# A fused attention and SwiGLU kernel: the output weights loaded by neighbouring rows, the wide weight columns in one transfer each, and a new order of work

## The chip, the core and the metric

The kernel runs on one core of a Trainium2 chip. A core has TensorE (PE, the matrix engine; its weight loads are listed apart, as PEld), VectorE (DVE), ScalarE (ACT), GpSimd (POOL) and SyncE (SP), which each run their own list of instructions in order and wait for each other by semaphores. Transfers between the chip's main memory and the core's on-chip memory are issued from SP, ACT or POOL and are carried out by 16 DMA engines. The metric is the device time of one execution in microseconds (us), lower being better.

## What is computed

For 8 batches and 8 heads, 576 positions and a head dimension of 64, attention with a forget gate; its result, rearranged to 4608 tokens of 512 values, goes through a gated feed-forward block of width 1536:

```python
log_f = np.log(np.clip(f, 0.0001, 1.0))
cum = np.cumsum(log_f, axis=-1)
scores = scale * q @ k.T + cum[..., :, None] - cum[..., None, :]
scores = np.where(causal, -1e9, scores)
attn = softmax(scores)                      # over the keys
x = (attn @ v) transposed and reshaped to (4608, 512)
g, val = x @ w_gate, x @ w_val              # (512, 1536) each
out = (g * sigmoid(g) * val) @ w_out        # (1536, 512)
```

Inputs and output are float32. The matrix products are done in bfloat16 with float32 sums.

## The kernel before

Attention works on pairs of heads (`p`, 32 of them), each in two halves `g` of query blocks (blocks 0 to 3, and 4 to 8, of 64 rows). For a pair, k and q are loaded, cast to bfloat16 (`kb`, `qb`), turned by TensorE (`tx`) and copied out (`kt`, `qz`). TensorE forms scores into `sp`; VectorE adds the forget sums `cb`, takes the row minimum and writes `t` and `tm` (L652); ScalarE takes the exponential (`e`, `eo`, L672); GpSimd, and for the first pairs ScalarE too, divides by the row sum and writes `pk` (L708); `pk` is turned into `pT`, for the first eight pairs by TensorE through a `gv` bank (L743), later by a DMA transpose; TensorE multiplies by v (`vt`, L764) and the result is copied, already transposed, into `xT`, the input of the feed-forward block.

The feed-forward block goes by tiles of tokens: two of 256 tokens, seven of 512, then 256, 128 and 128. `gate` (L839) makes, for each piece of a tile, a bank of gate columns from `wg` and one of value columns from `wv`, with 512 values in a bank; ScalarE takes a tanh (`th`, L855), VectorE makes the gated product `hh` in two passes (L857, L860). `project` multiplies `hh` with `wo` and stores 128 tokens at a time. Each matmul of 128 output rows is issued as two of 64 columns of the stationary operand (`columns`, L201), so a pair of matmuls, each with its own weight load of 64 columns, makes one product. The stationary operand of a gate product is the weight `wt[:, ko, fc * P:fc * P + P]`, 128 neighbouring columns; the moving operand is `xT`, 512, 256 or 128 tokens wide. In `project` the stationary operand is `hh` and the moving one is `wo[:, fc, :]`.

The weights lie in three on-chip arrays for the whole run. `weights` (L814) issues their loads from POOL, which also casts them to bfloat16: `wg` and `wv` in four pieces of columns each (0 to 256, to 512, to 1024, to 1536), `wo` in three pieces of 512 rows. A row `fc*128 + p` of `w_out` goes to partition `p` of chunk `fc`.

All of the order is fixed before the run. Every step is given to a planner (`Plan`) with the engines that may do it and a cost for each, a priority, buffers, and for transfers a DMA cost (`dma`) and a share of the DMA engines (`pk`). `Plan.order` simulates the engines with these costs and writes out the instructions of each engine in the order that it found. Several constants steer it: `STARTUP` is the sequence of the loads of the first part, `AHEAD` and `BEHIND` say how far apart in that sequence a load may be issued, `SLACK` how long a buffer is held for an earlier user, and `NUDGE` shifts the priorities of single units of work (a: scores and softmax, f: gates, o: projections, q: preparations, v: v loads). These are orders and not waits: the instructions that come out wait for their data only.

Of the kernel before, what the change touches and what calls it, by code (L numbers as in the profile page):

```python
# [197 lines left out]
def columns(nc, out, lhsT, rhs, **kw):  # L198
    for h in range(2):
        c = slice(64 * h, 64 * h + 64)  # L200
        nc.tensor.matmul(out[c, :], lhsT[:, c], rhs, **kw)  # L201
# [8 lines left out]
def mm(*cols):  # L210
    return sum(max(29, c / 2.4 + 2.5) for c in cols)
# [3 lines left out]
def kernel(  # L215
# [11 lines left out]
    nc = tc.nc  # L227
# [4 lines left out]
    P = 128  # L232
# [31 lines left out]


    NHALF = 4
    NSELA = 4
    NSEL = 1
    CUT = QB * (HI[0] + 1)
    MOST = (("p", 1), ("o", 2), ("f", 3))  # L270
    AHEAD = 10
    BEHIND = 5
    BOTH = 8
    LATER = {"DVE": 100}
    SPARE = {"ACT": 400, "DVE": 700}
    FREE = 8
    SLACK = 400
    SOON = 8
    BACK = 4
    CBACK = 5  # L280
    STARTUP = "p0 q1 f9 v01 k0 p2 wv2 q0 v04 wv0 wg2 wg0 k2 v00 c3 c1 q3 q2 wv4 v02 p4 c2 v03 c4 wg4 v11 c5 wv8 wg8 v10 v14 p5 v13 wo4 p6 v12 c6 wo0 c7 p7 wo8 c0"
    HEAD = "00 10 20 30 11 01 31 21"


    NUDGE = "a0.0:-6 a1.0:-12.5 a10.0:1 a10.1:1.5 a12.0:-0.5 a13.0:0.5 a13.1:-1 a15.0:-1 a15.1:1 a16.0:-3 a17.0:-2 a17.1:-1.5 a18.0:-0.5 a21.0:-1 a21.1:-1 a22.1:0.5 a25.1:-1 a26.1:-1.5 a27.0:-1.5 a27.1:1 a29.0:2 a30.1:-1 a31.0:0.5 a31.1:0.5 a4.0:2.5 a4.1:2.5 a5.0:-1.5 a5.1:-1 a6.0:0.5 a6.1:1 a7.1:-0.5 a8.0:-1 a9.1:-0.5 f0:4 f1:2 f11:-4 f3:-5 f4:-3.5 f5:-4 f6:-2 f7:1 f8:9.5 f9:0.5 o0:-1 o1:-991 o10:-12.5 o11:3.5 o4:1 o5:-7 o6:-4.5 o8:1 o9:9 q0:-8.5 q1:-12 q10:-1.5 q11:-3 q12:-1.5 q13:-3 q14:-4 q15:-2 q16:-6 q17:1.5 q18:-4 q19:-2 q2:-10 q21:0.5 q24:0.5 q26:2.5 q27:0.5 q29:-2 q3:-9.5 q30:-4 q4:-7 q5:-5 q6:-1 q8:-1 v1:-5.5 v2:-2 v3:3.5 v4:1.5 v5:5.5 v6:0.5 v7:-5"

    WAIT = ""
    ORDER = [(int(u[0]), int(u[1])) for u in HEAD.split()]
# [7 lines left out]
    pl = Plan()  # L296
# [14 lines left out]
    wo = sb.tile([P, KF, DM], BF16)  # L311
# [31 lines left out]
    pl.most = {("gv", x): n for x, n in MOST}  # L343
    pl.slack = SLACK

# [3 lines left out]
    for h in range(2):  # L349
        nc.gpsimd.affine_select(  # L350
            out=maskf[64 * h:64 * h + 64, :], in_=maskf[64 * h:64 * h + 64, :],
# [113 lines left out]
    def prepare(p):  # L465
        s = first[p]
        if p < NHALF:
            prepare_parts(p)
# [54 lines left out]
    def load_parts(p):  # L523
        b, hp = divmod(p, NPB)
        pl.key(("cb", p), "cb", p)
        for name, x, a, z, r, n in parts(p):
# [4 lines left out]
            def load(e, u, fk=fk, src=(k if name == "k" else q), a=a, z=z, r=r, m=m):  # L531
# [79 lines left out]
    def scores(p, g):  # L611
# [3 lines left out]
        for n, bank in enumerate(BANKS[g]):  # L615
# [4 lines left out]
            def mult(e, bank=bank, sk=sk):  # L620
                sp, kt, qz, o = pl.buf(sk), pl.buf(("kt", p)), pl.buf(("qz", p)), 0
                for i, a, z in bank:
# [148 lines left out]
    def spread(p, g, pv):  # L771
# [5 lines left out]
        for a, z in ((0, cut), (cut, w)):  # L777
# [3 lines left out]
            def evac(e, a=a, z=z):  # L781
# [4 lines left out]
                full = [list(d) for d in src.ap]  # L786
                x = R if p >= NHALF else R // 2
                inner = [[1, QB // x], [QB // x, x]]
# [28 lines left out]
    def weights():  # L817
        def piece(engs, fn, reads, writes, *a, **kw):
            loads[writes[0]] = pl.op(engs, fn, reads, writes, *a, **kw)

        cuts = [0, 256, 512, 1024, 1536]
        for a, z in zip(cuts, cuts[1:]):
            for nm, wt, src in (("wg", wg, moe_w_gate), ("wv", wv, moe_w_val)):
                piece({"POOL": 600}, lambda e, wt=wt, src=src, a=a, z=z: nc.gpsimd.dma_start(
                    out=wt[:, :, a:z], in_=src[:, a:z].rearrange("(ko p) n -> p ko n", p=P)),
                    (), [(nm, n) for n in range(a // P, z // P)], 2 + a / 256, dma=5.1 * (z - a) + 880, pk=20 if z - a == 256 else 42)
        for c in range(0, KF, 4):
            piece({"POOL": 600}, lambda e, c=c: nc.gpsimd.dma_start(
                out=wo[:, c:c + 4, :], in_=moe_w_out[c * P:(c + 4) * P, :].rearrange("(ko p) n -> p ko n", p=P)),
                (), [("wo", n) for n in range(c, c + 4)], 7 + c / 4, dma=3500, pk=42)  # L830

    gates_of = {}

    def gate(t, tok, n):
        nf = 512 // n
        x0 = tok % NRING
        assert x0 + n <= NRING
        for u in range(KF // nf):
            fcs = range(u * nf, u * nf + nf)  # L839
            xs = [("x", hp, m) for hp in range(KD) for m in range(tok // QB, (tok + n) // QB)]  # L840
            pr = 1000 + t * 20 + u
            for nm, wt in (("wg", wg), ("wv", wv)):
                bk = (nm, t, u)
                pl.key(bk, "gv", line="f")

                def mult(e, wt=wt, bk=bk, fcs=fcs):
                    for j, fc in enumerate(fcs):
                        for ko in range(KD):
                            columns(nc, pl.buf(bk)[:, j * n:j * n + n], wt[:, ko, fc * P:fc * P + P],
                                    xT[:, ko, x0:x0 + n], start=ko == 0, stop=ko == KD - 1)  # L850
                o = pl.op({"PE": mm(*[n] * (KD * nf))}, mult, xs + [(nm, fc) for fc in fcs], [bk], pr, lat=220)
                gates_of[t] = o
            pl.key(("th", t, u), "th")
            pl.key(("hh", t, u), "hh")
            pl.op({"ACT": 487}, lambda e, u=u: nc.scalar.activation(pl.buf(("th", t, u)), pl.buf(("wg", t, u)), AF.Tanh, scale=0.5),  # L855
                  [("wg", t, u)], [("th", t, u)], pr - 5000, lat=120)
            pl.op({"DVE": 605}, lambda e, u=u: nc.vector.scalar_tensor_tensor(  # L857
                pl.buf(("th", t, u)), pl.buf(("th", t, u)), 1.0, pl.buf(("wg", t, u)), op0=ALU.add, op1=ALU.mult),
                [("th", t, u), ("wg", t, u)], [("u", t, u)], pr - 5000, lat=180)
            pl.op({"DVE": 605}, lambda e, u=u: nc.vector.tensor_mul(pl.buf(("hh", t, u)), pl.buf(("th", t, u)), pl.buf(("wv", t, u))),  # L860
                  [("u", t, u), ("th", t, u), ("wv", t, u)], [("hh", t, u)], pr - 5000, lat=100)
# [41 lines left out]
    for b in range(B):  # L903
        pl.key(("vt", b), "vt")
        load_v(b)
    weights()
    line = []
    for x in STARTUP.split():
        n = int("".join(c for c in x if c.isdigit()))
# [95 lines left out]
```

## Time and profile before

| what | value |
|---|---|
| median of 3 runs | 414.49 us (414.43 to 421.14) |
| the profiled execution | 415.21 us |
| its span, from the first to the last instruction | 413.4 us |
| PE, DVE, ACT, POOL busy | 95%, 81%, 78%, 66% of the span |
| granted TensorE clock | 1.0 throughout |

The profiled execution is 1.8 us longer than its span, which is what lies before and after the instructions, and 0.7 us above the median. The views used here are the page of the whole run, tables of busy time in chosen stretches, the waits of one engine put down to what ended them, the chain of work that ended last, the groups of instructions by line and shape, and the timeline. In a group's row, "busy" is the time in which at least one of the group was running, and "mean ns" the mean length of one; since the two matmuls of a pair run side by side and are pipelined, busy time divided by the count is much less than the mean.

### The profile page before, as it was taken

How to read it: one execution, taken by the hardware profiler on the slowest of the kernel's cores; microseconds unless marked ns; L12 is line 12 of the kernel's file. 1: busy time of each engine (PE TensorE's matmuls, PEld its weight loads, DVE VectorE, ACT ScalarE, POOL GpSimd, SP SyncE). 2: the span in 40 equal slices, each digit the busy share in tenths (PEclk: the TensorE clock that was granted, in tenths of full speed). 3: DMA queues.
4: the chain of work that ended last, by engine and by line, in shares of the span. 5: the costliest groups of instructions: out<-in, count | busy, mean ns of one | idle time of the engine just before them, and what ended most of it. 6: DMA issues, size and time to landing. Idle time of an engine off the chain costs nothing.

```text
span 413.4 us, 15350 instructions
## 1 busy us (share of the span) xinstructions
PE 392.5 (95%) x5848; PEld 269.3 (65%) x5848; DVE 333.2 (81%) x1270; ACT 320.5 (78%) x904; POOL 271.1 (66%) x475
## 2 busy tenths in 40 slices
PE   3988988889999999999999999999999999999996
PEld 2667878777666765567776666665566555568775
DVE  4799987798999789999998999899989952775232
ACT  5799988799999998979998897998899653332221
POOL 7679966699996887799789798878777340000000
PEclk9999999999999999999999999999999999999999
DMA  7999979879799999999999999978996744000211
GB/s 192 190 216 226 216 126 247 163 189 210 184 230 191 229 196 233 241 203 230 224 196 223 234 210 225 239 215 182 201 223 114 149 93 126 2 2 28 79 53 52
DMA packets 144026, 72.16 MB, mean 175 GB/s; under 512 B 117904, under 2 KB 131728, under 8 KB 143952
## 3 DMA queue, kind: packets, MB, share of 16 engines
q1 hardware_dynamic: 137856, 66.21, 74.4%
q0 software_dynamic: 5808, 4.72, 7.9%
q8 instruction: 45, 0.74, 0.8%
q14 instruction: 29, 0.24, 0.2%
q10 hardware_dynamic: 288, 0.26, 0.2%
HBM read 46.65 MB, written 9.58 MB: 136 GB/s over the span
## 4 chain that ended last, share of the span: by engine, by line
PE 81%; DMA 6%; DVE 5%; ACT 3%; issue 2%; POOL 1%; SPq 1%; POOLq 0%; ACTq 0%
PE gv L201 63%; PE sp L201 9%; PE tx L764 4%; PE tx L207 3%; DMA wg<-in_moe_w_gate_dram 3%; DVE t L652 3%; DMA kf<-in_k_dram 2%; PE gv L207 2%; DMA vf<-in_v_dram 1%; ACT eo L672 1%; ACT e L672 1%; SPq L533 1%; POOL vt L811 0%; DVE th L857 0%; ACT kt L509 0%
## 5 line engine op out<-in xcount | busy, mean ns | idle before, releaser
L652 DVE CUSTOM_DVE_ANT_0 t<-sp,cb 128x320 f32<-128x320 f32 (+7 forms) x272 | 121.7, 463 | 9.7 <-PE sp L201 5.1
L708 POOL TENSOR_SCALAR pk<-e,lr 128x512 bf16<-128x512 f32 (+3 forms) x189 | 101.5, 541 | 41.9 <-DVE lr L690 19.7
L201 PE MATMUL gv<-xT,wg 128*64 128x512 bf16 (+2 forms) x1152 | 112.7, 326 | 2.5 <-issue 1.4
L201 PE MATMUL gv<-xT,wv 128*64 128x512 bf16 (+2 forms) x1152 | 112.4, 326 | 0.1
L201 PE MATMUL gv<-wo,hh 128*64 128x512 bf16 (+1 forms) x888 | 106.5, 373 | 0.0
L857 DVE SCALAR_TENSOR_TENSOR th<-th,gv 128x512 f32<-128x512 f32 x108 | 73.9, 684 | 31.3 <-ACT th L855 30.5
L672 ACT ACTIVATE e<-t,tm 128x448 f32<-128x448 f32 (+4 forms) x160 | 88.9, 557 | 5.1 <-DVE tm L652 4.7
L855 ACT ACTIVATE th<-gv 128x512 f32<-128x512 f32 x108 | 64.3, 595 | 35.8 <-PE gv L201 35.2
L201 PE MATMUL sp<-kt,qz 128*64 128x512 bf16 (+7 forms) x640 | 77.9, 294 | 5.3 <-DVE tm L652 3.4
L708 POOL TENSOR_SCALAR pk<-eo,lr 128x256 bf16<-128x256 f32 (+3 forms) x128 | 70.4, 550 | 12.3 <-DVE lr L690 9.0
L201 PEld LDWEIGHTS <-wg 128*64 128x64 bf16 x1152 | 58.8, 110 | 30.0 <-issue 1.6
L201 PEld LDWEIGHTS <-wv 128*64 128x64 bf16 x1152 | 59.8, 110 | 27.4 <-issue 0.4
L860 DVE TENSOR_TENSOR hh<-th,gv 128x512 bf16<-128x512 f32 x108 | 73.7, 684 | 4.8 <-PE gv L201 1.8
L672 ACT ACTIVATE eo<-t,tm 128x256 f32<-128x256 f32 (+3 forms) x128 | 71.3, 558 | 4.3 <-DVE tm L652 3.1
L201 PEld LDWEIGHTS <-hh 128*64 128x64 bf16 x888 | 50.7, 110 | 31.3
L201 PEld LDWEIGHTS <-qz 128*64 128x64 bf16 x640 | 41.7, 113 | 23.0 <-issue 5.9
L884 ACT ACTIVATE ot<-gv 128x512 f32<-128x512 f32 (+1 forms) x34 | 19.9, 584 | 26.2 <-PE gv L201 26.0
L652 DVE DVE_READ_ACCUMULATOR2_ANT tm<- 128x1 f32 x432 | 35.7, 83 | 0.0
L652 DVE CUSTOM_DVE_ANT_0 t<-sp,cm,tm 128x64 f32<-128x64 f32 x128 | 34.4, 277 | 1.2 <-PE sp L201 0.3
L481 POOL TENSOR_SCALAR qb<-qf 72x1024 bf16<-72x1024 f32 x28 | 29.2, 1045 | 2.7 <-DMA qf<-in_q_dram 2.6
L672 ACT ACTIVATION_READ_ACCUMULATOR e<-t,tm 128x1 f32 x160 | 30.8, 193 | 0.0
L764 PE MATMUL tx<-pT,vt 128*64 128x320 bf16 (+4 forms) x448 | 29.6, 263 | 1.2 <-ACT pT L743 0.7
(73 smaller groups left out, 432.3 us busy)
## 6 DMA issues: line engine op xcount, KB each, us to landing
out_dram<-ot SPq DMA_DIRECT2D x35, 256.0 KB
vf<-in_v_dram SPq DMA_DIRECT2D x32, 256.0 KB
cb<-cum_f SPq DMA_DIRECT2D x56, 144.0 KB
kf<-in_k_dram SPq DMA_DIRECT2D x28, 288.0 KB
qf<-in_q_dram SPq DMA_DIRECT2D x28, 288.0 KB
wo<-in_moe_w_out_dram POOLq DMA_DIRECT2D x3, 512.0 KB, 7.0
vf<-in_v_dram SPq DMA_DIRECT2D x8, 128.0 KB
wv<-in_moe_w_val_dram POOLq DMA_DIRECT2D x2, 512.0 KB, 8.8
```

The lines of the kernel that those rows point to most:

```text
L201: nc.tensor.matmul(out[c, :], lhsT[:, c], rhs, **kw)
L207: nc.tensor.transpose(out[c, :], src[:, c], ident)
L481: eng[e].tensor_scalar(dst, src, -scale, 1.0, op0=ALU.mult, op1=ALU.mult)
L533: (nc.scalar if e == "ACT" else nc.sync).dma_start(out=pl.buf(fk)[m * u:m * u + m, :, 0:r * D], in_=src[b, h0:h0 + 2, a:z].rearrange("h (p ...
L652: nc.vector.tensor_tensor_reduce(out=pl.buf(tk)[:, a:z], in0=pl.buf(sk)[:, o:o + z - a], in1=pl.buf(("cm", p))[:, i, :] if own else pl.buf ...
L672: nc.scalar.activation(pl.buf(ek)[:, :L], pl.buf(tk)[:, :L], AF.Exp, bias=pl.buf(("tm", p, g))[:, 0, i:i + 1], scale=-1.0, accum_out=pl.bu ...
L708: eng[e].tensor_scalar(dst, src, r, 1.0, op0=ALU.mult, op1=ALU.mult)
L764: nc.tensor.matmul(xo[r, 0:QB * n], vt[:, c, 2 * hp + h, :], pT[:, a:a + n, 64 * h:64 * h + 64], start=(c == 0), stop=(c == nch - 1))
L855: pl.op({"ACT": 487}, lambda e, u=u: nc.scalar.activation(pl.buf(("th", t, u)), pl.buf(("wg", t, u)), AF.Tanh, scale=0.5), [("wg", t, u)], ...
L857: pl.op({"DVE": 605}, lambda e, u=u: nc.vector.scalar_tensor_tensor(pl.buf(("th", t, u)), pl.buf(("th", t, u)), 1.0, pl.buf(("wg", t, u)), ...
L860: pl.op({"DVE": 605}, lambda e, u=u: nc.vector.tensor_mul(pl.buf(("hh", t, u)), pl.buf(("th", t, u)), pl.buf(("wv", t, u))), [("u", t, u), ...
L884: nc.scalar.mul(pl.buf(ok)[:, a:z], pl.buf(bk)[:, 0:z - a], 0.5)
```

## The change

The rows of `w_out` are loaded by `r` neighbouring rows a partition (r = 2 in the first piece of 512 rows, 4 in the two others), so a partition reads 4 or 8 KB in one run in place of 2 KB. With that, partition `p` of chunk `fc` holds another row of `w_out` than before; the gate and value products are made to match it by taking, as stationary operand, every second or fourth column of a block of 256 or 512 columns, in place of 128 neighbouring ones. The gate and value columns 512 to 1536 are loaded in one transfer each in place of two, so POOL issues 9 weight transfers and not 11. The planner's DMA costs follow, and the constants of the order (AHEAD, BEHIND, SLACK, STARTUP, NUDGE) are new; they were planned with instruction fetches taken into account, though no code for that is in the kernel.

```diff
     NHALF = 4
+    WROWS = (2, 4, 4)
...
-    AHEAD = 10
-    BEHIND = 5
+    AHEAD = 8
+    BEHIND = 12
...
-    SLACK = 400
+    SLACK = 1150
...
-    STARTUP = "p0 q1 f9 v01 k0 p2 wv2 q0 v04 wv0 wg2 wg0 k2 v00 c3 c1 q3 q2 wv4 v02 p4 c2 v03 c4 wg4 v11 c5 wv8 wg8 v10 v14 p5 v13 wo4 p6 v12 c6 wo0 c7 p7 wo8 c0"
+    STARTUP = "q1 p0 f9 p2 v04 c0 k2 q0 c3 q3 k0 v01 v02 wg0 wv2 wv0 v03 c1 wg2 v00 q2 c2 p4 c5 c4 p5 c7 p6 wg4 wv4 p7 v11 wo4 v12 wo8 c6 v10 v14 v13 wo0"
...
-        cuts = [0, 256, 512, 1024, 1536]
+        cuts = [0, 256, 512, 1536]
...
-                    (), [(nm, n) for n in range(a // P, z // P)], 2 + a / 256, dma=5.1 * (z - a) + 880, pk=20 if z - a == 256 else 42)
+                    (), [(nm, n) for n in range(a // P, z // P)], 2 + a / 256, dma=5.1 * (z - a) + 880, pk=20 if z - a == 256 else 42 * (z - a) / 512)
         for c in range(0, KF, 4):
-            piece({"POOL": 600}, lambda e, c=c: nc.gpsimd.dma_start(
-                out=wo[:, c:c + 4, :], in_=moe_w_out[c * P:(c + 4) * P, :].rearrange("(ko p) n -> p ko n", p=P)),
-                (), [("wo", n) for n in range(c, c + 4)], 7 + c / 4, dma=3500, pk=42)
+            r = WROWS[c // 4]
+            piece({"POOL": 600}, lambda e, c=c, r=r: nc.gpsimd.dma_start(
+                out=wo[:, c:c + 4, :].rearrange("p (g r) n -> p g (r n)", r=r),
+                in_=moe_w_out[c * P:(c + 4) * P, :].rearrange("(g p r) n -> p g (r n)", p=P, r=r)),
+                (), [("wo", n) for n in range(c, c + 4)], 7 + c / 4, dma=2788 + 704 / r, pk=42 * r)
...
                         for ko in range(KD):
-                            columns(nc, pl.buf(bk)[:, j * n:j * n + n], wt[:, ko, fc * P:fc * P + P],
+                            r = WROWS[fc // 4]
+                            w = wt[:, ko, fc // r * r * P:(fc // r + 1) * r * P].rearrange("p (m r) -> p r m", r=r)[:, fc % r, :]
+                            columns(nc, pl.buf(bk)[:, j * n:j * n + n], w,
                                     xT[:, ko, x0:x0 + n], start=ko == 0, stop=ko == KD - 1)
```

The line of NUDGE, a list of some 120 shifts, is replaced by another of the same kind.

More of the change, by code (lines that the diff above doesn't have):

```diff
@@ L280 @@
     CBACK = 5
-    STARTUP = "p0 q1 f9 v01 k0 p2 wv2 q0 v04 wv0 wg2 wg0 k2 v00 c3 c1 q3 q2 wv4 v02 p4 c2 v03 c4 wg4 v11 c5 wv8 wg8 v10 v14 p5 v13 wo4 p6 v12 c6 wo0 c7 p7 wo8 c0"
+    STARTUP = "q1 p0 f9 p2 v04 c0 k2 q0 c3 q3 k0 v01 v02 wg0 wv2 wv0 v03 c1 wg2 v00 q2 c2 p4 c5 c4 p5 c7 p6 wg4 wv4 p7 v11 wo4 v12 wo8 c6 v10 v14 v13 wo0"
     HEAD = "00 10 20 30 11 01 31 21"
-    NUDGE = "a0.0:-6 a1.0:-12.5 a10.0:1 a10.1:1.5 a12.0:-0.5 a13.0:0.5 a13.1:-1 a15.0:-1 a15.1:1 a16.0:-3 a17.0:-2 a17.1:-1.5 a18.0:-0.5 a21.0:-1 a21.1:-1 a22.1:0.5 a25.1:-1 a26.1:-1.5 a27.0:-1.5 a27.1:1 a29.0:2 a30.1:-1 a31.0:0.5 a31.1:0.5 a4.0:2.5 a4.1:2.5 a5.0:-1.5 a5.1:-1 a6.0:0.5 a6.1:1 a7.1:-0.5 a8.0:-1 a9.1:-0.5 f0:4 f1:2 f11:-4 f3:-5 f4:-3.5 f5:-4 f6:-2 f7:1 f8:9.5 f9:0.5 o0:-1 o1:-991 o10:-12.5 o11:3.5 o4:1 o5:-7 o6:-4.5 o8:1 o9:9 q0:-8.5 q1:-12 q10:-1.5 q11:-3 q12:-1.5 q13:-3 q14:-4 q15:-2 q16:-6 q17:1.5 q18:-4 q19:-2 q2:-10 q21:0.5 q24:0.5 q26:2.5 q27:0.5 q29:-2 q3:-9.5 q30:-4 q4:-7 q5:-5 q6:-1 q8:-1 v1:-5.5 v2:-2 v3:3.5 v4:1.5 v5:5.5 v6:0.5 v7:-5"
+    NUDGE = "a0.0:4.5 a1.0:-17.5 a1.1:1.5 a10.1:0.5 a11.0:-1.5 a12.0:1 a13.0:-0.5 a14.0:-2.5 a14.1:0.5 a15.0:-1 a15.1:-0.5 a16.0:-3 a17.1:1.5 a19.0:0.5 a2.0:-3 a21.1:-1 a22.1:-0.5 a23.0:-1 a23.1:-1 a24.0:-0.5 a24.1:-1 a25.0:0.5 a26.0:-1.5 a26.1:1 a28.0:1 a28.1:-1 a3.0:1 a3.1:0.5 a31.0:8.5 a31.1:3.5 a4.0:-1.5 a4.1:4.5 a5.0:-1 a5.1:-2 a6.1:3 a8.0:1.5 a8.1:1.5 a9.1:2 f0:-1 f1:2.5 f10:1 f11:19.5 f2:10.5 f3:3 f4:-3.5 f5:-1.5 f6:-6.5 f7:-2.5 f8:-4 o0:-985 o10:4.5 o11:1 o2:5 o3:7 o4:0.5 o7:6 o8:4 q0:-27 q1:-51 q10:-1 q11:-2.5 q12:-1 q13:-4 q14:-4 q15:-5 q16:-6 q19:-2 q2:-27.5 q22:-1.5 q23:1.5 q25:2 q27:-1 q28:0.5 q29:-2.5 q3:-20.5 q30:1 q31:4 q4:-22 q5:-1.5 q7:-1.5 q8:2.5 v2:4.5 v3:1 v4:-2 v5:4 v7:0.5"
     WAIT = ""
```

## The prediction, made before the changed kernel was run

> **What bounds the kernel now.** I read the page first, then the busy time by stretches, PE's waits, and the chain of waits.
>
> ```profile
> span 413.4 us, 15350 instructions
> PE 392.5 (95%) x5848; PEld 269.3 (65%) x5848; DVE 333.2 (81%) x1270; ACT 320.5 (78%) x904; POOL 271.1 (66%) x475
> PE   3988988889999999999999999999999999999996
> ```
>
> PE (the digits are its busy tenths in 40 slices) is full from the tenth slice to the last but one and has holes before that. By stretches (columns: the stretch and its length, then busy time and instructions of PE, PEld, DVE, ACT, POOL):
>
> ```profile
> 0.00:30.00 30.00, 20.76 (x256) 14.73 (x257) 21.44 (x88) 22.67 (x71) 21.78 (x63) 1.00 0.99 197
> 30.00:100.00 70.00, 62.34 (x1339) 54.25 (x1340) 60.16 (x209) 62.16 (x169) 55.80 (x93) 1.00 0.96 197
> 100.00:410.00 310.00, 309.27 (x4262) 200.36 (x4256) 251.59 (x974) 235.17 (x665) 193.49 (x320) 1.00 0.80 168
> 410.00:413.40 3.40, 0.09 (x2) 0.00 (x0) 0.00 (x0) 0.51 (x2) 0.00 (x0) 1.00 0.23 77
> 40.00:50.00 10.00, 9.57 (x244) 8.78 (x243) 8.89 (x23) 9.04 (x20) 9.96 (x16) 1.00 1.20 226
> ```
>
> From 100 us on PE is idle 0.73 us in 310: no order can win anything there, and the amount of PE work is the same in both kernels (11683 rows on PE each, by a comparison of their instructions). What can be won lies in the first 100 us, where PE idles 9.24 us up to 30 and 7.66 us from 30 on. PE's waits name it (engine and line, what it waited for, total, times, longest):
>
> ```profile
> PE tx L207 <- ACT kb L560: 4.6, 1, 4.6
> PE sp L201 <- DVE tm L652: 3.4, 9, 1.0
> PE gv L201 <- issue: 1.4, 1, 1.4
> PE tx L207 <- issue: 1.4, 1, 1.4
> PE gv L201 <- DMA wg<-in_moe_w_gate_dram: 1.0, 2, 0.7
> ```
>
> The 4.6 us are the first operand of all, which has to be loaded in any order. Without them, 12.3 us of idle time are the ceiling of a better start. The chain of waits passes through the same places (start, length, what):
>
> ```profile
> 42.69 12.02 DMA wg<-in_moe_w_gate_dram
> 66.91 1.38 issue
> 74.14 1.44 issue
> ```
>
> **The change, part by part.** The sum is made against the profiled execution: a span of 413.4 us in a time of 415.21, which is 0.72 above the median of 414.49; at the end I take the saving off the median.
>
> *Instruction fetches.* "Issue" marks time in which PE waited for nothing that the profile shows. The two gaps last 1.38 and 1.44 us, 2.82 together, while PE's program comes in over a queue of its own (packets, MB, share of the DMA engines):
>
> ```profile
> q8 instruction: 45, 0.74, 0.8%
> ```
>
> That is 45 blocks of some 16 KB, and the gaps lie where the `wo` transfers are on their way:
>
> ```profile
> 58.16 0.80 POOL L828 DMA_DIRECT2D wo<-in_moe_w_out_dram  x1
> 60.07 0.74 POOL L828 DMA_DIRECT2D wo<-in_moe_w_out_dram  x1
> 74.69 0.80 POOL L828 DMA_DIRECT2D wo<-in_moe_w_out_dram  x1
> L201 PE MATMUL gv<-wo,hh x888: 272/379/384, 78.2 to 409.8; 128*64 128x512 bf16 x168, 128*64 128x256 bf16 x10
> ```
>
> So late blocks are a likely cause, though an inferred one. The change cannot lower the number of blocks, only their place beside other transfers. Bounds: -2.8 us if both gaps go, +2.8 if as many are added. I take half of the gain, **-1.4**. [...]
>
> *Two weight transfers fewer on POOL.* What an issue takes there, at two of today's 1 MB pieces, and the first of the divisions around them (start, length):
>
> ```profile
> 30.53 0.68 POOL L708 TENSOR_SCALAR pk<-e,lr 128x512 bf16<-128x512 f32 x1 [1.59 <-DVE lr L690]
> 33.42 0.80 POOL L824 DMA_DIRECT2D wg<-in_moe_w_gate_dram  x1
> 40.19 0.80 POOL L824 DMA_DIRECT2D wv<-in_moe_w_val_dram  x1
> ```
>
> Two issues are 1.6 us. From 40 to 50 us POOL is busy 9.96 of 10, and its divisions (`pk`) feed the transposes on PE, so part of this is on the path; in its idle stretches it is hidden. Bounds -1.6 and 0; I take **-0.8**.
>
> *Wide transfers and their landing.* The third gate piece (columns 512 on) goes out at 33.4 us now. In the new order both wide transfers, 2 MB each as read, follow the six divisions of the fifth unit of attention (they start at 30.5 us now), with only one cast between them; I put them at about 34 and 36 us. PE works in order: the first product on these columns waits for the whole 2 MB, and behind it the scores of the next pairs, VectorE's and ScalarE's supply. By counting matmuls, at the paces shown further below, that product has 20.3 us of PE work ahead of it (18.9 now, where it starts at 42.9 us), so it is wanted near 44, its value product 5 us later. How that product starts now, and how long all gate pieces take:
>
> ```profile
> 42.89 1.06 PE L201 MATMUL gv<-xT,wg 128*64 128x256 bf16 x16 [0.30 <-DMA wg<-in_moe_w_gate_dram]
> DMA to landing us min/median/max: 8.0/9.3/12.0
> ```
>
> Within 10 us of the issue, and nothing is late. At the pace of the last two 1 MB pieces (40.19 to 54.71, the end of the 12.02 us in the chain: 14.5 us for 2 MB), the gate columns land at 48.5, 4.5 us late, and the value columns at 63, another 8.5 us late. Bounds: -1.0 (today's wait for `wg` goes) and +13. I take **+1.0**: eight pieces cost PE only 1.0 us now, and all of it is DMA time that attention work can cover. The longer runs of `wo` are costed at 0: its first product comes at 78.2 us, 18 us after the first two pieces go out (the row above), at a place in PE's order that hardly moves; if that cover were gone, a landing like the 12.0 us would show.
>
> *Stationary operands with a step of 2 or 4.* No weight load of the trace has a step, so this is bounded. The products are paced thus:
>
> ```profile
> 388.81 1.06 PE L201 MATMUL gv<-xT,wg 128*64 128x128 bf16 x32
> 389.71 1.06 PE L201 MATMUL gv<-xT,wv 128*64 128x128 bf16 x32
> 376.68 1.04 PE L201 MATMUL gv<-xT,wv 128*64 128x256 bf16 x16
> 377.55 1.04 PE L201 MATMUL gv<-xT,wg 128*64 128x256 bf16 x16
> 83.49 0.46 PE L207 MATMUL tx<-ident,qb 72*64 72x72 bf16 x16
> 83.75 1.06 PE L201 MATMUL gv<-wo,hh 128*64 128x512 bf16 x8
> ```
>
> From start to start, a pair of matmuls takes 0.90/16 = 56 ns at 128 tokens, 0.87/8 = 109 ns at 256, and 0.26/8 = 32.5 ns in the transposes, each with two loads of 64 columns. So two loads need at most 32.5 ns, and the matmuls hide them; at 512 tokens all the more. The pairs that could be uncovered:
>
> ```profile
> L201 PE MATMUL gv<-xT,wg 128*64 128x256 bf16 x288 | 19.1, 273 | 2.5 <-issue 1.4 <-DMA wg<-in_moe_w_gate_dram 1.0
> L201 PE MATMUL gv<-xT,wg 128*64 128x128 bf16 x192 | 6.3, 219 | 0.0
> ```
>
> With as many for `wv`, these are 288 pairs at 256 tokens and 192 at 128. If a step halves the load rate, two loads take 65 ns: 192 x 9 = +1.7 us. If the rate falls with the step, chunks 4 to 11 (step 4, two thirds) need 130 ns: 128 x 74 + 192 x 21 + 64 x 9 ns = +14.1 us. The nearest rows are other engines' copies of bfloat16, `kt` read with a step of 96 values, `pT` without:
>
> ```profile
> L509 ACT COPY kt<-tx 128x576 bf16<-128x576 bf16 x22 | 13.9, 632 | 1.0 <-PE tx L207 1.0
> L743 ACT COPY pT<-gv 128x1024 bf16<-128x1024 bf16 x7 | 7.0, 1002 | 0.1
> L511 DVE COPY kt<-tx 128x576 bf16<-128x576 bf16 x6 | 4.5, 754 | 0.6 <-PE tx L207 0.5
> L743 DVE COPY pT<-gv 128x1024 bf16<-128x1024 bf16 x9 | 6.2, 685 | 0.1
> ```
>
> ScalarE takes 1.10 and 0.98 ns a value, so a step costs it next to nothing; VectorE 1.31 and 0.67, a factor of two. I take **0**: even the factor of two stays under the cover but for the last two tiles. [...]
>
> *The new order otherwise.* Of the 12.3 us, 2.8 are fetches and 1.0 the `wg` waits; the other 8.5 are waits for softmax, casts and copies. VectorE, ScalarE and POOL are busy 80% and more of the time from 30 to 100 us, so a different order can shift these waits more than remove them. Bounds: -8.5 and, mirrored, +4 for new ones (the size of VectorE's 3.4 and the like); I take a quarter, **-2.1**. At the end, the last value product stands closer to the last projection than now. The last `hh` needs, after its gate product, one pass of ScalarE and two of VectorE:
>
> ```profile
> L855 ACT ACTIVATE th<-gv 128x512 f32<-128x512 f32 x108 | 64.3, 595 | 35.8 <-PE gv L201 35.2
> L857 DVE SCALAR_TENSOR_TENSOR th<-th,gv 128x512 f32<-128x512 f32 x108 | 73.9, 684 | 31.3 <-ACT th L855 30.5
> ```
>
> These 2.0 us lie beside the value product (16 pairs of 56 ns, 0.9 us) and four pieces of the projection (16 pairs of 109 ns, 1.7 us). I take 0; without that cover the end would come up to 2 us later.
>
> Sum: -1.4 - 0.8 + 1.0 + 0 - 2.1 = -3.3 us: a span of 410.1 and, off the median, **411.2 us**.
>
> **The rivals.** *The start packs much tighter:* fetch gaps, `wg` waits and half of the rest go, 2.8 + 1.0 + 4.2 + 1.6 for POOL = 9.6 us, so 405 us. For it: all of that idle time lies ahead of 100 us. Against: VectorE, ScalarE and POOL are nearly full in the same slices. *The holes only move:* PE's gaps come back at other places, and 414.5 us stays. For it: same work, same blocks, same bytes. *The wide transfers land late,* half of their upper bound, 6.5 in place of 1.0: 416.7 us, up to 423 at the full 13. For it: the 12.02 us in the chain. *The stepped loads are slow* (the case on the other side): from a load time that grows with the step, the tiles of 256 and 128 tokens lose their cover; at 14.1 us the time is 411.2 + 14.1 = 425.3. It passes the 2% line (422.8) when two loads with a step of 4 take some 122 ns. For it: VectorE's rows. Against: ScalarE's, and a cover of 56 to 109 ns over 32.5.
>
> **How the numbers follow.** Chances: forecast 0.38, holes only move 0.17, tighter start 0.16, late transfers 0.14 (0.05 of it past the 2% line), slow loads 0.15. A change of 2%, 8.3 us, is about what a measurement of this kernel can tell from no change. Faster by more: 0.16. Slower by more: 0.05 + 0.15 = 0.20. Within: 0.64. The range, 404.5 to 423, leaves out the slow loads but for their mildest form, the worst late transfers and a fifth of the tighter starts, together 0.2. Within the likeliest case alone it is 408 to 413.5.
>
> **What would show it.** In the changed profile PE's idle time before 100 us should be some 3 us below 16.9, and about 0.7 between 100 and the end of its matmuls. The issue gaps show the fetches, the waits for `wg` and `wv` the wide transfers. The pace of the 128-token products tells the loads: 56 ns a pair if a step is free, 65 at half rate, 130 at a quarter. A loss in the steady part after 100 us would make the whole reading wrong, for I find nothing there that the change touches.

## The result, and the profile after

| kernel | median | lowest to highest | ratio to before, 95% interval |
|---|---|---|---|
| before, on the same chip | 416.94 us (4 executions) | 414.43 to 421.14 | 1 |
| changed | 431.88 us (4 executions) | 430.63 to 433.59 | 1.0382 [1.0283, 1.0481] |

The change makes the kernel slower by 3.8%, where the forecast was 411.2 us with a range up to 423. The ratio leaves out a disturbed execution of the kernel before, so it is not quite that of the medians. The profiled execution took 431.5 us, of which the span is 429.7.

From the page of the changed kernel: the span, the busy time, PE's busy tenths in 40 slices, and the granted clock in tenths.

```profile
span 429.7 us, 15367 instructions
PE 399.1 (93%) x5848; PEld 307.9 (72%) x5848; DVE 336.6 (78%) x1275; ACT 319.6 (74%) x902; POOL 267.5 (62%) x470
PE   4975369999999999999999999999999999999996
PEclk9986669999999999999999999999999999999999
```

PE runs 5848 matmuls as before. A hole has come in from the fourth slice to the sixth (each is 10.7 us), and the clock falls to six tenths in it. By stretches of the changed kernel (the stretch and its length, then busy time and instructions of PE, PEld, DVE, ACT and POOL, then the granted clock, the DMA share and GB/s):

```profile
0.00:30.00 30.00, 20.60 (x240) 14.29 (x241) 20.78 (x87) 21.47 (x67) 22.25 (x65) 0.94 0.83 193
30.00:100.00 70.00, 52.23 (x1051) 46.19 (x1052) 47.88 (x160) 46.99 (x124) 40.29 (x66) 0.85 0.75 158
100.00:410.00 310.00, 309.80 (x4223) 233.73 (x4221) 262.46 (x1023) 246.21 (x704) 204.96 (x341) 1.00 0.84 175
40.00:50.00 10.00, 3.98 (x58) 3.14 (x56) 3.02 (x9) 3.02 (x6) 8.68 (x12) 0.67 0.86 162
```

After 100 us PE idles 0.20 us in 310, less than before. What is left to do at 100 us takes 329.7 us here and took 313.4 before: the 16.3 us by which the two spans differ are work that was not done in the first 100 us, 1291 matmuls in place of 1595. From 40 to 50 us PE does 58 where it did 244; VectorE and ScalarE are idle as well. So no engine is at its limit there: PE waits, and the others with it. PE's waits in the changed kernel (engine and line, what it waited for, total, times, longest):

```profile
PE gv L201 <- DMA wg<-in_moe_w_gate_dram: 11.1, 2, 6.0
PE tx L207 <- POOL ls L378: 4.8, 1, 4.8
PE gv L201 <- DMA wv<-in_moe_w_val_dram: 4.6, 1, 4.6
PE gv L201 <- issue: 0.3, 1, 0.3
PE sp L201 <- DVE tm L653: 1.1, 2, 0.8
```

Three waits for the weights, 15.7 us together, where there was 1.0; the other terms of the forecast (issue, `tm`) have shrunk. The timeline shows where they stand. First PE's products of the first tiles, then POOL's issues of the second gate piece and the two wide transfers (start, length, what, and in brackets the idle time before it and what ended it):

```profile
33.01 0.30 PE L201 MATMUL gv<-xT,wg 128*64 128x256 bf16 x2
38.40 1.71 PE L201 MATMUL gv<-xT,wg 128*64 128x256 bf16 x14 [5.09 <-DMA wg<-in_moe_w_gate_dram]
40.39 1.80 PE L201 MATMUL gv<-xT,wv 128*64 128x256 bf16 x16
42.83 0.28 PE L201 MATMUL gv<-xT,wg 128*64 128x256 bf16 x2
49.13 1.71 PE L201 MATMUL gv<-xT,wg 128*64 128x256 bf16 x14 [6.03 <-DMA wg<-in_moe_w_gate_dram]
52.84 0.28 PE L201 MATMUL gv<-xT,wv 128*64 128x256 bf16 x2
57.73 1.71 PE L201 MATMUL gv<-xT,wv 128*64 128x256 bf16 x14 [4.61 <-DMA wv<-in_moe_w_val_dram]
```

```profile
28.79 0.80 POOL L825 DMA_DIRECT2D wg<-in_moe_w_gate_dram  x1
40.40 0.79 POOL L825 DMA_DIRECT2D wg<-in_moe_w_gate_dram  x1 [6.41 <-PE gv L201]
42.50 0.74 POOL L825 DMA_DIRECT2D wv<-in_moe_w_val_dram  x1 [0.46 <-PE gv L201]
```

Three things are odd here. A product of 16 matmuls starts with 2 and then waits for a weight, three times. The first gate product needs columns 0 to 255, which have long landed (its first two matmuls ran), yet it goes on at 38.40, just as the second piece lands, issued at 28.79 for columns 256 to 511. And POOL, which should only send out the wide gate transfer, stands still for 6.41 us until PE has made a product: nothing in the arithmetic asks that a load of columns 512 to 1535 wait for products of columns 0 to 255. The chain of waits of the changed kernel ties them together (start, length, what):

```profile
28.79 9.56 DMA wg<-in_moe_w_gate_dram
38.40 1.72 PE gv L201 x14
40.40 0.79 POOL wg L825
...
42.50 15.19 DMA wv<-in_moe_w_val_dram
57.73 1.72 PE gv L201 x14
```

A load holds up a product, the product holds up the next load, and that load the next product. The instruction lists of the two kernels, with the semaphores that each instruction waits for, show it as well. In the old kernel no load of `wg` or `wv` waits, and a product waits once, at its first weight load (row 506). In the changed one:

```text
POOL   70 L825 DMACopy wg<-in_moe_w_gate_dram 128x4x1024 [waits PE]
POOL   72 L825 DMACopy wv<-in_moe_w_val_dram 128x4x1024 [waits PE]
PE    542 L201 Ldweights wg [waits DMASW0]
PE    546 L201 Ldweights wg [waits DMASW3]
```

The second and third stopped products, at 42.83 and 52.84, are those of columns 256 to 511, whose own pieces landed before; by the list they wait for the two wide transfers, that is for columns from 512 on.

The waits are put in by a layer below the planner. The places fit one explanation: the layer compares the addresses that instructions read and write, and where a read has a step, it is compared by the whole stretch from its first address to its last, or against the whole stretch of the load, and not column by column. In `wg`, a partition holds 1536 columns of the first 128 rows (`ko` = 0), then of the next, up to `ko` = 3. A load of columns 256 to 511 spans, taken as one stretch, from column 256 of `ko` = 0 to column 511 of `ko` = 3. Columns 0 to 255 of `ko` = 0 lie ahead of that stretch, those of `ko` = 1 inside: two matmuls free, then a wait, as seen. That the layer works so is inferred; what follows tests what it would make of the time.

### The profile page after: what moved, and what is told of

The parts are those of the page before. It is cut to its first block, busy times and chain, and to the rows that moved or that the text cites. A ratio compares the mean times of both kernels' runs of the same rounds, so it can differ in the third digit from the quotient of the medians.

```text
span 429.7 us, 15367 instructions
## 1 busy us (share of the span) xinstructions
PE 399.1 (93%) x5848; PEld 307.9 (72%) x5848; DVE 336.6 (78%) x1275; ACT 319.6 (74%) x902; POOL 267.5 (62%) x470
## 4 chain that ended last, share of the span: by engine, by line
PE 84%; DMA 8%; POOL 4%; ACT 2%; issue 1%; DVE 0%; POOLq 0%; DVEq 0%; ACTq 0%
PE gv L201 64%; PE sp L201 9%; PE tx L765 5%; PE tx L207 4%; DMA wv<-in_moe_w_val_dram 4%; DMA wg<-in_moe_w_gate_dram 2%; DMA pT<-pk 2%; PE gv L207 2%; PE gv L426 1%; POOL pk L709 1%; ACT e L673 1%; ACT pT L744 1%; ACT eo L673 1%; POOL qb L563 1%; POOL vt L812 0%
## 5 line engine op out<-in xcount | busy, mean ns | idle before, releaser
L709 POOL TENSOR_SCALAR pk<-e,lr 128x128 bf16<-128x128 f32 (+3 forms) x191 | 102.8, 542 | 51.4 <-DVE lr L691 20.5
L653 DVE CUSTOM_DVE_ANT_0 t<-sp,cb 128x512 f32<-128x512 f32 (+7 forms) x272 | 121.4, 463 | 16.3 <-PE sp L201 7.6
L201 PE MATMUL gv<-xT,wv 128*64 128x512 bf16 (+2 forms) x1152 | 117.3, 331 | 5.0 <-DMA wv<-in_moe_w_val_dram 4.6
L201 PEld LDWEIGHTS <-wg 128*64 128x64 bf16 x1152 | 73.0, 130 | 29.3 <-DMA wg<-in_moe_w_gate_dram 11.5
L673 ACT ACTIVATE e<-t,tm 128x576 f32<-128x576 f32 (+4 forms) x160 | 88.6, 555 | 3.9 <-DVE tm L653 3.4
L201 PEld LDWEIGHTS <-wv 128*64 128x64 bf16 x1152 | 73.7, 130 | 23.0 <-DMA wv<-in_moe_w_val_dram 4.8
L201 PE MATMUL sp<-kt,qz 128*64 128x64 bf16 (+7 forms) x640 | 79.4, 297 | 1.4 <-DVE tm L653 1.1
L201 PEld LDWEIGHTS <-hh 128*64 128x64 bf16 x888 | 57.4, 110 | 25.6
L709 POOL TENSOR_SCALAR pk<-eo,lr 128x256 bf16<-128x256 f32 (+1 forms) x124 | 67.5, 544 | 8.3 <-DVE lr L691 5.6
L765 PEld LDWEIGHTS <-vt 128*64 128x64 bf16 x448 | 25.5, 112 | 7.6 <-issue 2.7
```

The source lines that it names most:

```text
L653: nc.vector.tensor_tensor_reduce(out=pl.buf(tk)[:, a:z], in0=pl.buf(sk)[:, o:o + z - a], in1=pl.buf(("cm", p))[:, i, :] if own else pl.buf ...
L673: nc.scalar.activation(pl.buf(ek)[:, :L], pl.buf(tk)[:, :L], AF.Exp, bias=pl.buf(("tm", p, g))[:, 0, i:i + 1], scale=-1.0, accum_out=pl.bu ...
L709: eng[e].tensor_scalar(dst, src, r, 1.0, op0=ALU.mult, op1=ALU.mult)
L765: nc.tensor.matmul(xo[r, 0:QB * n], vt[:, c, 2 * hp + h, :], pT[:, a:a + n, 64 * h:64 * h + 64], start=(c == 0), stop=(c == nch - 1))
```

## The experiments

The theory: the step in the weight reads makes the products and the loads of other columns of one array wait for each other, and these waits are the loss. The rivals: the steps slow the weight loads themselves; the wide transfers land late because they are wide; or the new order is bad. All ratios are to the kernel before on the chip of that run, with 95% intervals; here they stand together.

| order | reads | weights in | other | ratio to before |
|---|---|---|---|---|
| old | plain | one array | the kernel before again | 0.9998 [0.9961, 1.0034] |
| old | plain | an array a piece | | 0.9999 [0.9947, 1.0051] |
| old | step 2 | an array a piece | | 1.0000 [0.9928, 1.0073] |
| old | step 2, 4, 4 | an array a piece | | 1.0042 [1.0006, 1.0078] |
| old | step 2, 4, 4 | one array | | 1.0407 [1.0324, 1.0490] |
| new | step 2, 4, 4 | one array | the change | 1.0382 [1.0283, 1.0481] |
| new | step 2, 4, 4 | two arrays, cut at column 512 | | 1.0179 [1.0104, 1.0254] |
| new | step 1, 4, 4 | one array | | 1.0086 [1.0052, 1.0120] |
| new | step 2, 4, 4 | an array a piece | | 1.0060 [1.0027, 1.0093] |
| new | step 2 | an array a piece | | 1.0024 [0.9986, 1.0062] |
| new | plain | one array | | 1.0034 [1.0002, 1.0065] |
| new | plain | one array | wide transfers halved | 1.0050 [1.0006, 1.0095] |

**An array for each piece.** The changed kernel, with the same order, steps and transfers; only the arrays are separate, so that no piece can be taken for another.

```diff
-    wg = sb.tile([P, KD, DF], BF16)
-    wv = sb.tile([P, KD, DF], BF16)
+    CUTS = [0, 256, 512, 1536]
+    wg, wv = ({a: sb.tile([P, KD, z - a], BF16, name=f"{nm}{a}") for a, z in zip(CUTS, CUTS[1:])} for nm in ("wg", "wv"))
...
+                            a = max(x for x in wt if x <= fc * P)
-                            w = wt[:, ko, fc // r * r * P:(fc // r + 1) * r * P].rearrange("p (m r) -> p r m", r=r)[:, fc % r, :]
+                            w = wt[a][:, ko, fc // r * r * P - a:(fc // r + 1) * r * P - a].rearrange("p (m r) -> p r m", r=r)[:, fc % r, :]
```

> The changed kernel with the same order, the same steps of 2 and 4 and the same transfers, but each piece of w_gate and w_val (columns 0 to 256, to 512, to 1536) in an on-chip array of its own. Theory A, waits that the data do not need: a read with a step from the one big array is taken by the recording layer to overlap the columns of other pieces, so products wait for later pieces and POOL's later loads wait for products. With separate arrays these waits are gone: PE's waits for wg and wv fall from 15.7 us to under 4 us, the wide transfers are issued near 34 and 36 us in place of 40.4 and 42.5, the granted clock in the first 100 us is back near 1.0, and the time is 408 to 416 us. Theory B, 2 MB transfers are simply too late for this order: PE's waits for wg and wv stay above 8 us and the time above 422. Theory C, weight loads with a step cost time themselves: waits shrink, but the pace of the 256- and 128-token products stays slow and the time stays above 420.

Measured: 415.93 us, 1.0060. Of the 3.8%, 3.2 are gone. The products and the wide transfers in its timeline, PE's and POOL's, and its waits:

```profile
33.58 1.11 PE L201 MATMUL gv<-xT,wg 128*64 128x256 bf16 x16
34.75 1.06 PE L201 MATMUL gv<-xT,wv 128*64 128x256 bf16 x16
38.92 1.06 PE L201 MATMUL gv<-xT,wg 128*64 128x256 bf16 x16 [2.30 <-DMA wg<-in_moe_w_gate_dram]
```

```profile
34.23 0.79 POOL L825 DMA_DIRECT2D wg<-in_moe_w_gate_dram  x1
35.79 0.74 POOL L825 DMA_DIRECT2D wv<-in_moe_w_val_dram  x1
```

```profile
PE gv L201 <- DMA wg<-in_moe_w_gate_dram: 2.3, 1, 2.3
PE gv L201 <- issue: 1.3, 1, 1.3
```

In the instruction list of this kernel no load of `wg` or `wv` waits, and the first product of each piece waits for that piece alone. The first product runs through. The wide transfers leave at 34.2 and 35.8, where the forecast put them (34 and 36), and the one wait left is that of the second gate piece, by the product that needs it. In the same stretch, this kernel and then the changed one:

```profile
30.00:64.00 34.00, 29.89 (x661) 26.76 (x661) 30.33 (x107) 29.82 (x82) 28.46 (x48) 1.00 1.07 219
```

```profile
30.00:64.00 34.00, 17.42 (x280) 14.09 (x280) 13.46 (x44) 13.92 (x36) 13.42 (x22) 0.70 0.72 152
```

Of the 16.58 us that PE idles in the second, 15.73 are the three waits; and while it is busy it does 16 matmuls in a us against 22, at a mean clock of 0.70 against 1.00.

**Plain reads, the rest as changed.** The new order and the wide transfers, without neighbouring rows and steps:

```diff
-                out=wo[:, c:c + 4, :].rearrange("p (g r) n -> p g (r n)", r=r),
-                in_=moe_w_out[c * P:(c + 4) * P, :].rearrange("(g p r) n -> p g (r n)", p=P, r=r)),
+                out=wo[:, c:c + 4, :], in_=moe_w_out[c * P:(c + 4) * P, :].rearrange("(ko p) n -> p ko n", p=P)),
...
-                            w = wt[:, ko, fc // r * r * P:(fc // r + 1) * r * P].rearrange("p (m r) -> p r m", r=r)[:, fc % r, :]
+                            w = wt[:, ko, fc * P:fc * P + P]
```

> The changed kernel with the same order and the same wide transfers, but w_out by one row a partition as before and the gate and value products on 128 neighbouring columns, all in the one big array. A: without a step the recording layer sees that the pieces do not overlap, the extra waits are gone as with separate arrays, and the time is within 2 us of that run, 408 to 416. B: still above 422. C: faster than the run with separate arrays by what the stepped loads cost, by 1 to 14 us, and paced at 56 ns a pair of 128-token matmuls.

Measured: 414.77 us, 1.0034. Its waits and the first stretches:

```profile
PE gv L201 <- issue: 2.0, 2, 1.0
PE gv L207 <- issue: 1.3, 2, 0.9
...
PE gv L201 <- DMA wg<-in_moe_w_gate_dram: 0.6, 1, 0.6
```

```profile
0.00:30.00 30.00, 21.84 (x240) 15.04 (x241) 21.17 (x87) 21.76 (x68) 22.28 (x65) 1.00 0.87 196
30.00:100.00 70.00, 65.05 (x1386) 57.77 (x1387) 64.38 (x227) 62.49 (x174) 55.52 (x93) 1.00 0.97 202
```

The instruction list of this kernel has none of the extra waits either. The order and the wide transfers are not the loss, and they are no gain: the gaps named issue are back with 3.3 us, at other places.

**Steps alone, in the old order,** with one array and with an array for each of its four pieces. The first edit is the step in `wo`'s loads and in the products, as in the change; the second adds the separate arrays.

```diff
+    WROWS = (2, 4, 4)
...
-                            columns(nc, pl.buf(bk)[:, j * n:j * n + n], wt[:, ko, fc * P:fc * P + P],
+                            r = WROWS[fc // 4]
+                            w = wt[:, ko, fc // r * r * P:(fc // r + 1) * r * P].rearrange("p (m r) -> p r m", r=r)[:, fc % r, :]
+                            columns(nc, pl.buf(bk)[:, j * n:j * n + n], w,
```

> The kernel before with its own order and its four pieces of columns, with one thing added: w_out by 2 or 4 rows a partition and the steps that this needs in the gate and value products, in the big arrays. A: the extra waits appear here too. The first gate product waits for the piece of columns 256 to 512 (landed by then in the old order, so little), the third, fourth and fifth wide loads wait for products, and the fourth piece is wanted for the third; PE's waits for wg and wv rise from 1.0 to 4 to 15 us and the time to 418 to 432. B and any theory that blames the new order or the wide transfers alone: as the kernel before, 413 to 417. C: 2 to 14 us above it without any new wait for wg or wv.

> As the run of the kernel before with steps added, with each of the four pieces of w_gate and w_val in an array of its own. A: the waits of that run are gone again and the time is within 2 us of the kernel before, 413 to 418. C: what is left above the kernel before is the cost of the stepped loads by themselves, 2 to 14 us, seen in the pace of the 128-token products (56 ns a pair if a step is free, 65 at half rate).

Measured: 431.76 us, 1.0407, and 415.18 us, 1.0042. The profiled execution with one array, at 435.14 us the longest of the four, shows the same waits: PE stands 9.9 us for `wv` and `wg`, within the 4 to 15 expected, and POOL stands still before the third gate piece (PE's largest wait of the two, then POOL's row):

```profile
PE gv L201 <- DMA wv<-in_moe_w_val_dram: 8.4, 2, 4.7
```

```profile
40.15 0.80 POOL L825 DMA_DIRECT2D wg<-in_moe_w_gate_dram  x1 [6.29 <-PE gv L201]
```

With separate arrays neither wait is there. The steps bring the loss in the old order too, and separate arrays take nearly all of it away there too. So it needs neither the new order nor the wide transfers.

**Two arrays, cut at column 512.** The wide transfers write arrays of their own here, while the first two pieces still share one.

```diff
-    wg = sb.tile([P, KD, DF], BF16)
-    wv = sb.tile([P, KD, DF], BF16)
+    CUTS = [0, 512, 1536]
+    wg, wv = ({a: sb.tile([P, KD, z - a], BF16, name=f"{nm}{a}") for a, z in zip(CUTS, CUTS[1:])} for nm in ("wg", "wv"))
```

> The changed kernel with its order and its steps, w_gate and w_val in two arrays each, cut at column 512. The wide loads then write an array that no earlier product has read, so POOL does not wait for products; the first products still wait for the second 256-column piece of the same array. This parts the two kinds of extra wait. If POOL's wait before the wide loads carries most of the loss, the wide loads go out near 36 us (a first product that still waits some 5 us for the piece of columns 256 to 512 delays nothing behind them on POOL), PE's waits for wg and wv are 5 to 8 us in place of 15.7, and the time is 418 to 423 us. If the early products' wait carries it, the time stays at 425 to 430. If neither kind matters by itself, 414 to 417.

Measured: 420.78 us, 1.0179. Its first product and the first wide transfer, on PE and POOL:

```profile
33.25 0.30 PE L201 MATMUL gv<-xT,wg 128*64 128x256 bf16 x2
39.23 1.70 PE L201 MATMUL gv<-xT,wg 128*64 128x256 bf16 x14 [5.67 <-DMA wg<-in_moe_w_gate_dram]
```

```profile
34.55 0.79 POOL L825 DMA_DIRECT2D wg<-in_moe_w_gate_dram  x1
```

POOL no longer waits and sends at 34.55; the first product still stops after two matmuls, 5.67 us. So the first wait comes apart from the others: against the kernel with an array a piece it costs 1.2 points of per cent (1.0179 against 1.0060), some 5 us; all that comes later costs 2.0 more (1.0382 against 1.0179), some 8 us. The intervals of the three do not overlap, but only just. What comes later is two things, POOL's halt and the waits of the products of columns 256 to 511 for the wide transfers; this cut ends both, so it does not tell what each costs alone.

**A step of 1 in the first 512 columns.** One number, `WROWS`, with the planner's costs kept: products of the columns that are wanted while loads are still going out then read plainly, in one array.

```diff
-    WROWS = (2, 4, 4)
+    WROWS, COST = (1, 4, 4), (2, 4, 4)
```

> The changed kernel with one number different: w_out's first piece of 512 rows by one row a partition in place of two, so the products on the first 512 gate and value columns read 128 neighbouring columns; the planner's costs are kept, so the order is the same, and everything is in the one big array, with step 4 for the other 1024 columns. If the loss comes from waits that only reads with a step cause, and only while other pieces of the same array are still to come, then it is gone: the wide piece is the last one and its readers need it anyway. 414 to 417 us, PE's waits for wg and wv under 4 us. If steps as such, or the wide transfers, cost the time, it stays above 422.

Measured: 417.47 us, 1.0086; 0.9 us of waits for `wg`, none for `wv`, and the wide transfers leave at 34.4 and 36.0. The time is a little above the 414 to 417 expected. Two thirds of the columns are still read by steps of 4, and most of the loss is gone: it is not the number of stepped reads that costs, but where they meet loads. Why some 2 us more are left here than with plain reads (1.0086 against 1.0034, with intervals that overlap) is open; the pace of the loads with a step of 4, shown below, accounts for 0.7 us.

**The wide transfers in halves,** in the kernel with plain reads (two of 512 columns one after the other for each of 1024).

> The run without steps in the one big array (new order, plain reads), with each wide transfer issued as two of 512 columns, one right behind the other. It shows what one wide transfer is worth against two narrow ones in this order. If the saved POOL issues and longer runs count, it is 1 to 3 us slower than the run with wide transfers (414.8), 416 to 418. If the product that can start on 512 columns gains more than that, 412 to 414. No difference beyond 1 us: the transfers are covered either way.

Measured: 415.16 us, 1.0050 [1.0006, 1.0095], against 1.0034 for the wide ones: no difference that can be told.

**The kernel before once more,** to show what two copies of one kernel differ by.

> The kernel before, unchanged, as a control on the same chip and for a profile beside the others: a ratio of 1.000 within 0.4%, and PE's idle time before 100 us of some 17 us, against 13.1 us in the run with the new order and plain reads. If that run's 13.1 us is no better than this one's, the new order saves nothing at the start.

Measured: 413.40 us, 0.9998. Its first two stretches:

```profile
0.00:30.00 30.00, 21.01 (x256) 15.21 (x257) 21.44 (x88) 22.67 (x71) 22.13 (x63) 1.00 1.01 201
30.00:100.00 70.00, 64.03 (x1378) 55.36 (x1379) 61.42 (x213) 63.87 (x172) 57.42 (x95) 1.00 0.98 199
```

PE idles 15.0 us before 100 us here (8.99 + 5.97), less than the 17 expected, and 13.1 in the new order with plain reads (8.16 + 4.95). The executions of the two kernels overlap (412.19 to 419.06 here, 413.09 to 417.24 there), so these 1.9 us of one execution each are not seen in the times.

**What is left of the steps.** Three kernels for the remaining 0.4 to 0.6%: the old order with separate arrays and plain reads, the same with a step of 2 everywhere, and the changed kernel with separate arrays and a step of 2 everywhere.

```diff
-    WROWS = (2, 4, 4)
+    WROWS = (2, 2, 2)
```

> The kernel before with each piece of wg and wv in an array of its own, plain reads, nothing else changed. Theory A (the 0.4% that the old order paid with steps and separate arrays is the slower loads with a step of 4): no step here, so the ratio is 1.000 +- 0.002 and the 128-token products keep 56 ns a pair. Theory B (the price lies in the separate arrays, for example in other addresses): 1.003 to 1.005, as with steps.

> The kernel before with separate arrays and a step of 2 in all three pieces of wo and all gate and value products. Theory A (step 4 costs, step 2 is free): all 128-token products at 56 ns a pair and a ratio of 1.000 +- 0.002. Theory B (separate arrays cost): 1.003 to 1.005. Theory C (any step costs, in products hidden from the pace): 1.002 to 1.005 with the kernel with separate arrays alone at 1.000.

> The changed kernel with separate arrays and a step of 2 everywhere, planned with the same costs. The changed kernel with separate arrays and steps of 2 and 4 took 1.006 of before, with plain reads 1.0034. Theory A: the steps of 4 were the difference, so 1.003 to 1.004 here, 56 ns a pair, and the new order with wide transfers still wins nothing. Rival: the longer runs of wo are worth something once no step of 4 is paid, so below 1.000.

Measured: 0.9999, 1.0000 and 1.0024, each uncertain by 0.4 to 0.7%. That fits the theory that only the step of 4 costs something, but the intervals overlap those of its counterparts, so the times don't prove it. The pace of the products shows that it costs, and how much of the time that is. Old order with separate arrays, steps of 2, 4 and 4, and then the same with 2 everywhere (products of 128 tokens, 16 pairs a row, columns from 0 on in the first two rows of each):

```profile
389.51 1.06 PE L201 MATMUL gv<-xT,wg 128*64 128x128 bf16 x32
390.41 1.06 PE L201 MATMUL gv<-xT,wv 128*64 128x128 bf16 x32
391.30 1.16 PE L201 MATMUL gv<-xT,wg 128*64 128x128 bf16 x32
392.29 1.15 PE L201 MATMUL gv<-xT,wv 128*64 128x128 bf16 x32
393.27 1.16 PE L201 MATMUL gv<-xT,wg 128*64 128x128 bf16 x32
```

```profile
390.12 1.09 PE L201 MATMUL gv<-xT,wg 128*64 128x128 bf16 x32
391.01 1.09 PE L201 MATMUL gv<-xT,wv 128*64 128x128 bf16 x32
391.91 1.09 PE L201 MATMUL gv<-xT,wg 128*64 128x128 bf16 x32
```

From start to start a step of 2 takes 0.89 us for 16 pairs, 56 ns a pair as without a step; a step of 4 takes 0.98 to 0.99, some 61.5 ns. For the 128 pairs with a step of 4 that is 0.7 us. The old order with steps of 2, 4 and 4 lost 0.42% [0.06, 0.78], 1.7 us; where the rest of that comes from, if it is more than noise, no run shows. The longer runs in which `w_out` is read bring nothing that can be told: in the old order with separate arrays, 1.0000 with two rows a partition and 0.9999 with one.

## Why the prediction was wrong

*The reading of what bounds the kernel* held: all of the movement lies in the first 100 us, and the 310 us after them stay full. The closing test of the prediction, a loss in that steady part, did not come up.

*Wide transfers and their landing* is the step that failed. It took the issue times from the order alone, "at about 34 and 36 us", and let each product wait for its own columns only; it was set at +1.0 with a bound of +13, and the waits came to 15.7. With the waits that the data need, the step was about right: the wide transfers leave at 34.2 and 35.8 with separate arrays, at 34.0 and 35.6 with plain reads, PE does not wait for them at all, and halves gain nothing. What is left is a wait for the second gate piece, 2.3 and 0.6 us in these two, 0.6 to 4.1 us over the five profiled kernels in the new order without the extra waits. What was missing is that the wide gate load was held up to 40.40 by a product, that product by another piece's load, and the products of columns 256 to 511 by the wide loads. A slip in the sum changes nothing: with the first product 4.5 us late, a value product wanted 5 us after 44 and a landing at 63 would be another 9.5 us late, not 8.5, and the bound +14, still under 15.7. The description of the kernel before carried the same mistake when it said that the instructions wait for their data only: for the loads and products of `wg` and `wv` that was so with plain reads, and the change ended it.

*Stationary operands with a step* asked only how fast such a load goes. There it was nearly right, 0 taken and up to +14.1 allowed: a pair takes 56 ns at a step of 2, as without one, and 61.5 ns at 4; 128 pairs by 5.6 ns are 0.7 us, and the old order with steps and separate arrays took 1.0042 [1.0006, 1.0078], 1.7 us. It did not ask what else a new form of read touches. The rival of slow loads, 425.3 us, came nearest to the time, but by another mechanism: it needed some 122 ns for two loads, and they fit in 61.5.

*Instruction fetches* (-1.4) gave nothing: the issue gaps, 2.8 us before, are 3.3 in the new order with plain reads and 1.3 with separate arrays; they move. That they come from fetches no run tested. In the changed kernel itself 0.3 is left, but PE stands still for other reasons there. *Two weight transfers fewer* (-0.8) gave nothing that can be told: with the two issues put back, by halves, the time was 415.16 us against 414.77. *The new order otherwise* (-2.1) has its size in PE's idle time (1.9 us less before 100 us with plain reads) and not in the measured time, 1.0034 [1.0002, 1.0065]. Without the extra waits the rival "the holes only move" would have been right.

One thing may hide the 1.9 us. In the five kernels in the new order without the extra waits, the mean granted clock of an execution was below 0.99 in 25 of 52 executions; in the kernel before it was so in none of 88 (the lowest was 0.992). The profiled execution with plain reads was one of the two of its kernel at 1.00, and its fastest. In the two profiled executions of these kernels that had a mean clock below 0.99, halved transfers (0.983) and separate arrays with steps of 2 (0.987), the granted clock was 0.89 and 0.94 up to 30 us, 0.95 in both from 30 to 100, and 1.00 after that. So the new order often pays in clock at the start; that this eats what it saves in idle time is likely, and not shown.

What the forecast lacked altogether is the granted clock. In the changed kernel it was 0.50 from 35.5 to 42 us, from 45.5 to 52 and from 55.7 to 62.4: each time from some 2 us into one of the three waits (5.1, 6.0 and 4.6 us) until 3 to 5 us after its end. In the stretches of 10 us from 30 to 60 us that makes 0.67 to 0.76, and after the first wait 16 matmuls of 256 tokens took 1.80 us where they take 1.06 with separate arrays. The runs show the same drop behind less: in the changed kernel the clock was 0.50 from 25 to 28 us too, where the two holes just before lasted 0.76 and 0.38 us, and with the wide transfers halved it was 0.89 over the first 30 us, in which no product waits for a weight. And a wait of 2.30 us with separate arrays left it at 1.00, as PE's first wait in the kernel before did, with 4.61 us. What sets the clock is open.

What stays open: how the layer compares addresses is not shown, only where its waits fall and that they go with separate arrays or plain reads. And no kernel of this study is faster than the one before; of those in the new order, the one with separate arrays and steps of 2, at 1.0024 [0.9986, 1.0062], is the nearest.

## What to carry to other kernels

When a change alters how an array is read, by a step or another pattern, compare the waits in the instruction lists before and after, not only the order: here the two added lines on POOL's loads stood there before anything ran. Pieces of one array that are loaded and used at different times are safest as arrays of their own: with steps of 2 and 4 that took the ratio from 1.0382 to 1.0060 in the new order, and from 1.0407 to 1.0042 in the old. A load that waits for a product (POOL for 6.41 us here), or a product that stops after its first matmuls (2 of 16), was the sign of it in the timeline.

## What the runs showed of the hardware

In these runs a weight load of 64 columns with a step of 2 values of bfloat16 took as long as one without, 110 ns on the mean; with a step of 4 it took longer, 134 to 148 ns in the products told apart below. The mean length of one, in the old order with plain reads, with a step of 2 and with steps of 2, 4 and 4 (the three kernels with separate arrays; line, engine, shape and count, busy time, mean ns):

```profile
L201 PEld LDWEIGHTS <-wv 128*64 128x64 bf16 x1152 | 60.4, 110 | 26.8
```

```profile
L201 PEld LDWEIGHTS <-wv 128*64 128x64 bf16 x1152 | 63.9, 110 | 23.6
```

```profile
L201 PEld LDWEIGHTS <-wv 128*64 128x64 bf16 x1152 | 67.0, 129 | 22.2
```

The 129 ns are a mean over loads with a step of 2, a third of them, and of 4; in the changed kernel, where the two can be told apart by product, the 32 loads of `wg` for 128 tokens from 404.2 us on, with a step of 2, take 110 to 111 ns, and the 32 from 406.2 us on, with a step of 4, 134 to 148. In the pace only the step of 4 shows through, and only in products of 128 tokens, 61.5 ns a pair against 56: with 256 tokens, 8 pairs take 0.87 us from start to start with a step of 4 as without, and with 512 the mean matmul takes 380 ns against 379.

In the changed kernel, where three holes of 4.6 to 6.0 us lie within 25 us, the granted clock was 0.76, 0.67 and 0.67 in the three stretches of 10 us from 30 us on; from 60 to 70 us it was 0.88, and only then 1.00 again. With the holes came slower work around them: from 30 to 64 us PE idled 16.6 us, and did 16 matmuls in a busy us against 22 with separate arrays.
